# A Fourier filter and an ELU MLP on one core: order of the start's loads, place of one batch's sums, and the last unit's output

## The chip, the cores and the metric

The kernel runs on one core of a Trainium2 chip. A core has a matrix engine (TensorE, PE, with its weight loads as PEld), VectorE (DVE), ScalarE (ACT), GpSimd (POOL) and SyncE (SP), each with its own stream of instructions carried out in order, and 16 DMA engines. A DMA is issued from the stream of SP, ACT or POOL. The metric is the device time of one execution in microseconds (us); lower is better. The time before is the median of three runs, 2563.66 us (2563.2 to 2564.88).

## What is computed

`x` is (8, 3008, 256), `filt_r` and `filt_i` are (1505, 256), `moe_w_in` is (256, 2048) and `moe_w_out` (2048, 256); the two weights come in as 64-bit floats, the rest and the output as 32-bit floats.

```python
X = np.fft.rfft(x, axis=1)
F = (filt_r + 1j * filt_i)[None, :, :]
y = np.fft.irfft(X * F, n=x.shape[1], axis=1)        # (8, 3008, 256)
t = y.reshape(24064, 256)
h = t @ w_in                                          # (24064, 2048)
g = np.where(h > 0.0, h, np.exp(np.minimum(h, 0.0)) - 1.0)
out = g @ w_out                                       # (24064, 256)
```

## The kernel before

**The MLP is the bulk.** The 24064 tokens are 8 batches of 6 units (m = 0 to 5), and a unit has 4 quads (q = 0 to 3, a quarter of the 2048 hidden columns each): 192 quads in a row. In the text "quad 5" is the sixth quad of the whole run; batch 0's tokens are quads 0 to 23. The two matrix products use a seven-product scheme of Strassen's kind, so a quad has seven "up" steps (`up_steps`, matmuls of L572; they are issued as 1, 2, 6, 5, 7, 3, 4) and seven "down" steps (`down_steps`, L654), each four matmuls; the downs belong to the quad before. Between them ACT copies and exponentiates (L583, L589, L590) and DVE adds and takes the maximum (L580, L594, L630 to L634). A step that needs another product's bank waits for DVE's add of L580.

**The order is written out by hand.** The loop at the very end of the kernel issues ups and downs of a quad in a fixed pattern, "UUDUDDU" and then "DUUDUDD"; in a quad that is in the set `opens` a down goes first. Everything else is put in by `at(quad, place, function, ...)`: place 2 comes after the third step, 3 after the fifth, 0 in the middle and 1 at the end of the quad. What a function issues then stands at that place in the stream of each engine that it uses.

**The transform of the next batch runs inside the MLP of this one.** The sequence of 3008 is taken as 47 x 64. For batch b the steps are:

- `x_load` (six chunks, on SP): seven DMAs of x and of a table for each chunk.
- `x_unit` (L222, L223): two DVE operations per chunk, a sum and a difference of 128 x 512 elements.
- `a_unit` (L236): 32 matmuls for two chunks, into all four PSUM banks that the ups use too, with four evictions on ACT (L240).
- `z_write` (L310, SP): two DMAs per chunk into a scratch tensor z in DRAM; `z_read` (L316, SP): four DMAs for each of two groups of frequencies, which read z back transposed, once all of it has been written.
- `b_unit` (L385) on two groups that were read; the products with the filter (`re_mult`, `im_mult` and so on, on DVE; the filter is fetched by POOL at L326); `bi_unit` (L457); `y_write` (SP) into a scratch tensor yd.
- `tn_read` and `y_read` (L480, L491, SP) fetch a unit's inputs of the last stage, `n_unit` (L524) makes the unit's tokens, and `n_sums` (L549) the sums that the seven-product scheme needs.

Batch 0 has no MLP to hide in. Its transform and the conversion of the first weights are the start of the kernel, some 85 us: the x chunks come in by `x_load_first`, and `a_first(c)` (L279, 16 matmuls in two lots, with four evictions on ACT, L286) puts them into tiles zt. `t_first` (L298, evictions L299) transposes these, `b_first` makes the spectrum (L332) and the products with the filter (L336 to L339 on DVE), `bi_first` the way back, and the results go out and come back through DRAM (yd) to the first `n_unit` (L506).

A weight piece k is 512 KB of 64-bit floats. `w_fetch(k)` brings it in, and `step(k)` turns it to 32-bit floats: `w_split(k)` (two DVE operations), `w_float(k)` (four ACT operations), and then `w_join(k-1)` (three or four DVE operations, and `w_sums` with four more after each second piece). In the stream of ACT the evictions of `a_first` stand where they are called among the `step`s.

**SP's order in the start** is: piece 0, x chunks 0 to 2, piece 4, piece 5, chunks 3 and 4, piece 6, chunk 5, `once` (tables), `gs` (tables), piece 7. Piece 5 goes to a filter buffer, piece 6 and 7 into x buffers that `a_first` has freed. POOL fetches pieces 1 to 3 and rearranges the filter in DRAM.

**The output of a unit** is joined from the down products by seven DVE additions (L670): three at once, then two in `c_unit` and two in `o_unit`, in the order p7, c21, c12, c22. Then `o_unit` turns it with two DVE transposes (L693), one for each half k of the tokens, and issues the output DMAs (L703), 16 for most units and 24 for unit 0 of a batch. They go through SP; for the last unit, (7, 5), through SP and ACT in turn. Of the four blocks of a unit's output, c11 and c21 make up the half k = 0, c12 and c22 the half k = 1.

Of the kernel before, what the change touches and what calls it, by code (L numbers as in the profile page):

```python
# [28 lines left out]
B = 8  # L29
# [4 lines left out]
NXC = H // XC  # L34
# [99 lines left out]
def kernel(  # L134
# [9 lines left out]
    nc = tc.nc  # L144
# [497 lines left out]
    def down_steps(b, m, q):  # L642
        h = half(m)
        g = g_of.pop((b, m, q))
        if q == 0:
            po_of[b, m] = [psO.tile([P, 2, 256], FP32, tag="po%d" % i, name="po%d" % i) for i in range(4)]
        po = po_of[b, m]
        k = {}

        def step(n):  # L650
            i, u = PLACE[n]
            for a in range(2):

                nc.tensor.matmul(po[i][:, u, 0:h], w_out[q][:, COMBO[n], a, :], g[n][:, a, :],  # L654
                                 start=q == 0 and a == 0 and n in (1, 3, 6, 4), stop=True, skip_group_check=True)
            if q == 3 and n == 7:
                for i in range(2):
                    t = k[i] = kp.tile([P, 2, 256], FP32, tag="k%d" % i, name="k%d" % i)
                    nc.scalar.activation(out=t[:, :, 0:h], in_=po[i][:, :, 0:h], func=AXT.Copy)

        def tail():
            if q != 3:
                return
            p1, p5 = (k[0][:, u, 0:h] for u in range(2))
            p35, p7 = (k[1][:, u, 0:h] for u in range(2))
            c = kp.tile([P, 2, 512], FP32, tag="c", name="c")
            (c11, c12), (c21, c22) = ((c[:, i, 0:h], c[:, i, h:2 * h]) for i in range(2))

            def add(o, i0, i1):
                nc.vector.tensor_tensor(out=o, in0=i0, in1=i1, op=ALU.add)  # L670

            add(p35, p35, p5)
            add(c12, po[2][:, 1, 0:h], p1)
            add(c11, po[2][:, 0, 0:h], p1)
            rest = [(p7, p7, c12), (c21, po[3][:, 0, 0:h], p7), (c12, c12, p35), (c22, p7, p5)]
            cs_[b, m] = c, lambda i: [add(*r) for r in rest[i:i + 2]]

        return [(lambda n=n: step(n)) for n in DOWNS], tail

# [1 line left out]

    def c_unit(b, m):
        cs_[b, m][1](0)

    def o_unit(b, m):
        c, join = cs_.pop((b, m))
        join(2)
        o = op.tile([P, 16, 2, 32], FP32, tag="o", name="o")  # L690
        n = 7 if m == 0 else 8
        for k in range(2):
            nc.vector.transpose(out=o.rearrange("p (j k) e s -> p j k e s", k=2)[:, 0:n, k],  # L693
                                in_=c[:, :, k * half(m):(k + 1) * half(m)].rearrange("p e (j s) -> p j e s", s=32))

        o = o.rearrange("p (u f k) e s -> p u f k (e s)", u=4, f=2)
        queues = itertools.cycle((nc.sync, nc.scalar) if (b, m) == (B - 1, 5) else (nc.sync,))
        for k in range(2):
            for u, w, i in ((0, 3, 1), (3, 1, 0)) if m == 0 else ((0, 4, 4 * m),):
                for f in range(1 if i == 0 else 2):  # L700
                    n1 = N1 - i if f else i
                    for a in range(4):
                        next(queues).dma_start(raw(out, b * N + n1 + 32 * N1 * k,  # L703
                                                   [[N1 * D, 32], [-D if f else D, w], [1, 64]], 64 * a),
                                               o[ts(a, 32), u:u + w, f, k])

# [2 lines left out]
    def w_fetch(k, queue=nc.gpsimd):  # L711
        q, j = divmod(k, 4)

        if k in (3, 4, 14, 15):
            wd = t2[:, k % 11 - 3].rearrange("p u d -> p (u d)")
        elif k == 10:
            wd = t1p.tile([P, XC, D], FP32, tag="t1", name="wd").rearrange("p u d -> p (u d)")
        elif k in (6, 7, 8, 9):
            wd = xp.tile([P, 2, 2, D], FP32, tag="xc", name="wd").rearrange("p k u d -> p (k u d)")
        else:  # L720
            wd = fbufs[{5: 0, 11: 0, 12: 1, 13: 2}.get(k, k)].rearrange("p c u d -> p (c u d)")
        wd = wds[k] = wd.bitcast(U32).rearrange("p (a w) -> p a w", w=2)
        if j < 2:
            srcs = [moe_w_in.bitcast(U32)[ts(j, P), ts(q, 1024)]]
        else:
            srcs = [moe_w_out.bitcast(U32)[ts(4 * q + 2 * (j - 2) + i, P), :] for i in range(2)]
        for i, s in enumerate(srcs):
            n = 512 // len(srcs)
            queue.dma_start(wd[:, ts(i, n), :].rearrange("p a w -> p (a w)"), s)
# [83 lines left out]
    with tc.manual_schedule():  # L813


        with tc.tile_pool(name="boot", bufs=1) as bp:
# [37 lines left out]
            def step(k):  # L854
                w_split(k)
                w_float(k)
                if k > 0:
                    w_join(k - 1)

            for k in range(3):  # L860
                step(k)
            w_fetch(5, nc.sync)
            for c in (3, 4):
                x_load_first(c)
            a_first(0)
            w_fetch(6, nc.sync)
            x_load_first(5)
            nc.sync.dma_start(once, once_d)
            nc.sync.dma_start(gs, gs_d)
            step(3)  # L870
            for c in (1, 2):
# [2 lines left out]
                    w_fetch(c + 6, nc.sync)  # L874
            step(4)
            a_first(3)
            step(5)
            step(6)
            for c in (4, 5):
                a_first(c)  # L880
            for g in range(NG):
                f_read_first(g, ff[:, g])
                if g in (1, 3):
# [83 lines left out]
        for b in range(B):  # L967
            t = (b - 1) * PER
            if b > 0:
                for c, s in enumerate((2, 2, 3, 3, 4, 4) if b == 1 else (0, 0, 3, 3, 4, 4)):  # L970
                    at(t + s, 0, x_unit, b, c)
                    if c % 2 == 0:
                        opens.add(t + s + 1)
                        at(t + s, 1, a_unit, b, c)
                    if c % 2:
                        for k in (c - 1, c):
                            at(t + s, 1, z_write, b, k)
                        if c == NXC - 1:
                            for k in range(2):
                                at(t + s, 1, z_read, b, k)  # L980
                        for k in (c - 1, c):
                            nb, nxt = (b, k + XBUFS) if k + XBUFS < NXC else (b + 1, k + XBUFS - NXC)
                            if nb < B:
                                at(t + s, 1, x_load, nb, nxt)
                for g in range(0, NG, 2):
                    s = t + 6 + 2 * g
                    opens.update((s + 1, s + 4))
                    for k in (g, g + 1):
                        at(s - 2, 1, f_read, b, k)
                        if g:  # L990
                            at(s - 1, 0, z_read, b, k)
                    at(s, 1, b_unit, b, g)
                    at(s + 1, 2, re_mult, b, g)
                    at(s + 1, 1, re_sums, b, g)
                    parts = ((0, 0), (0, 1), (1, 0), (1, 1))
                    early = 3 if g == 6 else 4
                    at(s + 2, 2, im_mult, b, g, *parts[:early])
                    at(s + 2, 1, im_mult, b, g, *parts[early:])
                    at(s + 2, 1, im_join, b, g)
                    at(s + 3, 2, im_sums, b, g)  # L1000
                    at(s + 3, 1, bi_unit, b, g)
                    at(s + 3, 1, y_write, b, g)
            for m, s in enumerate((23, 25, 29, 32, 36, 40)):
                if b > 0 or m > 0:
                    at(t + s - 2, 0, tn_read, b, m)
                    at(t + s - 2, 1 if m == 0 else 0, y_read, b, m)
                    if b == 0 and m == 1:
                        at(t + s, 1, n_unit, b, m)
                        at(t + s, 1, n_sums, b, m)
                    else:  # L1010
                        at(t + s, 0, n_unit, b, m)
                        for place, *parts in (((t + s, 0), 0, 1, 2), ((t + s + 1, 2), 3, 4)) if m == 0 else (
                                ((t + s, 0), 0, 1), ((t + s, 1), 2, 3, 4)) if m < 3 else (((t + s + 2, 2),),):
                            at(*place, n_sums, b, m, *parts)
                if b == 0 and m == 1:
                    at(1, 1, w_join, 13)
                at(t + PER + 4 * m + 5, 0, c_unit, b, m)
                at(t + PER + 4 * m + 6, 0, o_unit, b, m)
# [57 lines left out]
```

## Time and profile before

| | |
|---|---|
| time, median of three runs | 2563.66 us (2563.2 to 2564.88) |
| the profiled execution, its own time | 2561.82 us |
| its span, first to last instruction | 2560.0 us |
| granted clock of TensorE | 0.996 |
| first matmul of the MLP | 87.39 us |
| last matmul of the MLP ends | about 2551.6 us |
| DMA traffic in the start, 0 to 40 us | 218, 313, 341, 341 GB/s in the four stretches of 10 us |

The time of an execution is the span and what lies around it, here 1.82 us. Times in the views count from the start of the span. An engine's busy share is an average over the whole span: the start, the first quads of batch 0 and the end have limits of their own, so those have to be read from their own stretches. A hole in PE's work is told by the idle time in brackets before a row, with what ended it.

### The profile page before, as it was taken

How to read it: one execution, taken by the hardware profiler on the slowest of the kernel's cores; microseconds unless marked ns; L12 is line 12 of the kernel's file. 1: busy time of each engine (PE TensorE's matmuls, PEld its weight loads, DVE VectorE, ACT ScalarE, POOL GpSimd, SP SyncE). 2: the span in 40 equal slices, each digit the busy share in tenths (PEclk: the TensorE clock that was granted, in tenths of full speed). 3: DMA queues.
4: the chain of work that ended last, by engine and by line, in shares of the span. 5: the costliest groups of instructions: out<-in, count | busy, mean ns of one | idle time of the engine just before them, and what ended most of it. 6: DMA issues, size and time to landing. Idle time of an engine off the chain costs nothing.

```text
span 2560.0 us, 43969 instructions
## 1 busy us (share of the span) xinstructions
PE 2521.4 (98%) x16682; PEld 2162.5 (84%) x16682; DVE 2067.6 (81%) x3578; ACT 1545.2 (60%) x2715; POOL 156.0 (6%) x307
## 2 busy tenths in 40 slices
PE   6999999999999999999999999999999999999998
PEld 4788889888898888988889888888889888898887
DVE  6978887788878888788877888778897788876766
ACT  7766556655566556665566655566655665555554
POOL 4001000000000000000000000000100010000000
PEclk8999999999999999999999999999999999999999
DMA  9662223523233221433225231353213322110010
GB/s 283 184 183 69 56 46 80 130 60 71 48 102 95 70 66 40 128 80 74 50 53 141 67 76 36 77 123 80 66 38 84 88 62 63 38 44 18 20 27 17
DMA packets 229879, 200.56 MB, mean 78 GB/s; under 512 B 129398, under 2 KB 201990, under 8 KB 229668
## 3 DMA queue, kind: packets, MB, share of 16 engines
q1 hardware_dynamic: 214820, 168.44, 26.9%
q0 software_dynamic: 13488, 28.86, 4.0%
q8 instruction: 131, 2.15, 0.4%
q14 instruction: 80, 0.66, 0.1%
q10 hardware_dynamic: 1360, 0.46, 0.1%
HBM read 125.80 MB, written 78.12 MB: 80 GB/s over the span
## 4 chain that ended last, share of the span: by engine, by line
PE 97%; DMA 2%; DVE 1%; issue 0%; ACT 0%; SPq 0%; DVEq 0%
PE po L654 45%; PE phs L572 25%; PE phd L572 13%; PE pha L572 6%; PE psn L524 2%; PE psa L236 2%; PE pf L385 1%; PE pv L457 1%; DMA xc<-in_x_dram 1%; PE po L332 1%; DMA x<-in_x_dram 0%; PE po L298 0%; PE psr L332 0%; PE psa L279 0%; DMA t<-yd 0%
## 5 line engine op out<-in xcount | busy, mean ns | idle before, releaser
L654 PE MATMUL po<-g,wo 128*128 128x256 f32 (+1 forms) x5376 | 1317.6, 377 | 0.0
L654 PEld LDWEIGHTS po<-g,wo 128*128 128x128 f32 x5376 | 1010.7, 190 | 165.9 <-issue 49.8
L583 ACT ACTIVATE g<-phs 128x512 f32<-128x512 f32 (+1 forms) x576 | 338.6, 588 | 735.0 <-PE phs L572 732.9
L590 ACT ACTIVATE e<-e 128x512 f32<-128x512 f32 (+1 forms) x768 | 477.1, 621 | 24.3
L594 DVE SCALAR_TENSOR_TENSOR g<-e,g 128x512 f32<-128x512 f32 (+1 forms) x576 | 387.6, 673 | 13.5 <-ACT e L590 13.1
L580 DVE TENSOR_TENSOR g<-phd,g 128x512 f32<-128x512 f32 (+1 forms) x384 | 258.9, 674 | 165.8 <-ACT e L590 108.4
L572 PE MATMUL phs<-y,wi 128*128 128x256 f32 (+1 forms) x1536 | 387.5, 375 | 0.0
L572 PE MATMUL phd<-y,wi 128*128 128x256 f32 (+1 forms) x1504 | 380.3, 375 | 0.0
L589 ACT ACTIVATE e<-g 128x512 f32<-128x512 f32 (+1 forms) x576 | 354.5, 615 | 34.2 <-DVE g L580 26.6
L572 PEld LDWEIGHTS phs<-y,wi 128*128 128x128 f32 x1536 | 291.4, 190 | 33.2 <-ACT g L583 0.2
L572 PEld LDWEIGHTS phd<-y,wi 128*128 128x128 f32 x1504 | 284.8, 190 | 35.1 <-DVE g L580 2.7
L594 DVE SCALAR_TENSOR_TENSOR g<-e,phs 128x512 f32<-128x512 f32 (+1 forms) x192 | 129.8, 676 | 115.8 <-ACT e L590 115.8
L572 PE MATMUL phs<-yt,wi 128*128 128x256 f32 (+1 forms) x768 | 193.8, 375 | 0.9 <-ACT g L583 0.9
L572 PE MATMUL phs<-yb,wi 128*128 128x256 f32 (+1 forms) x768 | 193.9, 375 | 0.6 <-ACT g L583 0.6
L572 PE MATMUL pha<-yb,wi 128*128 128x256 f32 (+1 forms) x736 | 186.0, 375 | 0.0
L589 ACT ACTIVATE e<-phs 128x512 f32<-128x512 f32 (+1 forms) x192 | 112.2, 584 | 112.0 <-PE phs L572 112.0
L580 DVE TENSOR_TENSOR g<-pha,g 128x512 f32<-128x512 f32 (+1 forms) x192 | 129.5, 674 | 44.7 <-PE pha L572 44.6
L572 PEld LDWEIGHTS phs<-yt,wi 128*128 128x128 f32 x768 | 145.7, 190 | 17.9 <-ACT g L583 1.2
L572 PEld LDWEIGHTS phs<-yb,wi 128*128 128x128 f32 x768 | 143.1, 190 | 20.2 <-ACT g L583 1.0
L326 POOL DMA_DIRECT2D fall<-fp x224 | 110.1, 499 | 719.8 <-DVE r L430 694.6
L572 PEld LDWEIGHTS pha<-yb,wi 128*128 128x128 f32 x736 | 139.3, 190 | 16.7 <-ACT fall L394 0.2
L631 DVE TENSOR_TENSOR g<-g,g 128x512 f32<-128x512 f32 (+1 forms) x192 | 130.7, 681 | 6.7
(166 smaller groups left out, 2063.5 us busy)
## 6 DMA issues: line engine op xcount, KB each, us to landing
yd<-t SPq DMA_DIRECT2D x127, 192.0 KB
t<-yd SPq DMA_DIRECT2D x92, 256.0 KB
z<-t SPq DMA_DIRECT2D x84, 256.0 KB
fall<-fp POOLq DMA_DIRECT2D x224, 96.0 KB, 2.9
t<-z SPq DMA_DIRECT2D x224, 96.0 KB
out_dram<-o SPq DMA_DIRECT2D x632, 32.0 KB
xc<-in_x_dram SPq DMA_DIRECT2D x84, 128.0 KB
xc<-in_x_dram SPq DMA_DIRECT2D x161, 64.0 KB
```

The source lines that it names most:

```text
L236: nc.tensor.matmul(p[o:o + 64, u, :], w[r, u, o:o + 64], src[r, u, :], start=True, stop=True)
L326: nc.gpsimd.dma_start(t[32 * a:32 * a + 24].rearrange("p c u d -> p (c u d)"), fp[g, a].rearrange("q c u d -> q (c u d)"))
L332: nc.tensor.matmul(ps[:, u:u + w, :], table[k, v, :], r[k, u:u + w, :], start=n == 0, stop=n == len(rhs) - 1)
L524: nc.tensor.matmul(p[ts(c, 64), dh, ts(q, 64)], t[r, i - 4 * m, ds(dh * P + 64 * c, 64)], w[r, i - 4 * m, :], start=True, stop=True)
L572: nc.tensor.matmul(ps[:, a, 0:h], w_in[q][:, COMBO[n], a, :], y[n], start=start and a == 0, stop=True, skip_group_check=True)
L580: nc.vector.tensor_tensor(out=g[o], in0=i0, in1=i1, op=ALU.add)
L583: nc.scalar.activation(out=g[o], in_=i0, func=AXT.Copy)
L589: nc.scalar.activation(out=e, in_=src, func=AXT.Relu, scale=-1.0)
L590: nc.scalar.activation(out=e, in_=e, func=AXT.Exp, scale=-1.0)
L594: nc.vector.scalar_tensor_tensor(out=g[n], in0=es[n], scalar=1.0, in1=src, op0=ALU.subtract, op1=ALU.max)
L631: nc.vector.tensor_tensor(out=b12, in0=b22, in1=b12, op=ALU.subtract)
L654: nc.tensor.matmul(po[i][:, u, 0:h], w_out[q][:, COMBO[n], a, :], g[n][:, a, :], start=q == 0 and a == 0 and n in (1, 3, 6, 4), stop=True, ...
```

## The change

Three parts that don't touch one another.

**In the start,** SP issues x chunks 3, 4 and 5 right behind piece 4, then piece 5, `once`, piece 6, `gs`, and piece 7 as before. `a_first(4)` is called before `step(5)` and `a_first(5)` between `step(5)` and `step(6)`; before, both came after `step(6)`. The orders of PE and DVE are the same as before; ACT's is changed by the place of the evictions.

**In batch 1's transform,** the six chunks' `x_unit` run at quads 2, 3, 4, 4, 5, 5 instead of 2, 2, 3, 3, 4, 4, those of quad 5 at place 2 (after its third step) and not in the middle. `a_unit`, `z_write` and the following `x_load` go to quads 3, 4 and 5 instead of 2, 3 and 4, the first two `z_read` to the end of quad 5 instead of 4, and `opens` has 4, 5, 6 instead of 3, 4, 5 for them. `b_unit(1, 0)` stays at the end of quad 6. From batch 2 on nothing is different.

**In the last unit,** the order of the last four additions is p7, c12, c22 and then c21; the half k = 1 is turned and sent out first, then c21 is added and the half k = 0 turned and sent. The 16 output DMAs go through SP, ACT and POOL in turn (6, 5 and 5) instead of SP and ACT (8 and 8).

```diff
-            cs_[b, m] = c, lambda i: [add(*r) for r in rest[i:i + 2]]
+            if last(b, m):
+                rest = [rest[i] for i in (0, 2, 3, 1)]
+            cs_[b, m] = c, lambda i, n=2: [add(*r) for r in rest[i:i + n]]
...
+    def last(b, m):
+        return (b, m) == (B - 1, 5)
...
     def o_unit(b, m):
         c, join = cs_.pop((b, m))
-        join(2)
+        join(2, 1 if last(b, m) else 2)
...
-        for k in range(2):
+        ot = o.rearrange("p (u f k) e s -> p u f k (e s)", u=4, f=2)
+        queues = itertools.cycle((nc.sync, nc.scalar, nc.gpsimd) if last(b, m) else (nc.sync,))
+        def turn(k):
             nc.vector.transpose(out=o.rearrange("p (j k) e s -> p j k e s", k=2)[:, 0:n, k],
                                 in_=c[:, :, k * half(m):(k + 1) * half(m)].rearrange("p e (j s) -> p j e s", s=32))
-        o = o.rearrange("p (u f k) e s -> p u f k (e s)", u=4, f=2)
-        queues = itertools.cycle((nc.sync, nc.scalar) if (b, m) == (B - 1, 5) else (nc.sync,))
-        for k in range(2):
+        if not last(b, m):
+            turn(0)
+            turn(1)
+        for k in (1, 0) if last(b, m) else (0, 1):
+            if last(b, m):
+                if k == 0:
+                    join(3, 1)
+                turn(k)
...
             for k in range(3):
                 step(k)
+            for c in (3, 4, 5):
+                x_load_first(c)
             w_fetch(5, nc.sync)
-            for c in (3, 4):
-                x_load_first(c)
+            nc.sync.dma_start(once, once_d)
             a_first(0)
             w_fetch(6, nc.sync)
-            x_load_first(5)
-            nc.sync.dma_start(once, once_d)
             nc.sync.dma_start(gs, gs_d)
...
             step(4)
             a_first(3)
+            a_first(4)
             step(5)
+            a_first(5)
             step(6)
-            for c in (4, 5):
-                a_first(c)
...
-                for c, s in enumerate((2, 2, 3, 3, 4, 4) if b == 1 else (0, 0, 3, 3, 4, 4)):
-                    at(t + s, 0, x_unit, b, c)
+                when = (2, 3, 4, 4, 5, 5) if b == 1 else (0, 0, 3, 3, 4, 4)
+                for c in range(NXC):
+                    s = when[c]
+                    at(t + s, 2 if s == 5 else 0, x_unit, b, c)
+                    s = when[c | 1]
                     if c % 2 == 0:
                         opens.add(t + s + 1)
                         at(t + s, 1, a_unit, b, c)
```

More of the change, by code (lines that the diff above doesn't have):

```diff
@@ L704, in o_unit @@
                                                    [[N1 * D, 32], [-D if f else D, w], [1, 64]], 64 * a),
-                                               o[ts(a, 32), u:u + w, f, k])
+                                               ot[ts(a, 32), u:u + w, f, k])
     wds = {}
```

## The prediction

> **What bounds the kernel now.** I read the page's busy times first, then the chain of waits over the start, then the timelines of the three places that the change touches. TensorE (PE) is busy for 98% of the span, so a change can only win where PE stands still: the start, a few holes, the end.
>
> ```profile
> PE 2521.4 (98%) x16682; PEld 2162.5 (84%) x16682; DVE 2067.6 (81%) x3578; ACT 1545.2 (60%) x2715; POOL 156.0 (6%) x307
> ```
>
> The chain of waits of 0 to 90 us (start, length, what) shows the start hanging on x chunks until 39.55, then on PE:
>
> ```profile
> 15.10 12.66 DMA xc<-in_x_dram
> 27.78 11.77 DMA x<-in_x_dram
> 39.68 3.77 PE psa L279 x16
> 44.00 3.57 PE po L298 x31
> ```
>
> The windows (length, then busy times; last two: DMA share and GB/s) say why: the DMA engines are full. VectorE (DVE) is the full one later in the start:
>
> ```profile
> 30.00:40.00 10.00, 6.37 (x28) 5.84 (x28) 4.28 (x8) 6.31 (x13) 3.30 (x6) 0.50 1.06 341
> 70.00:80.00 10.00, 10.00 (x60) 4.96 (x55) 9.93 (x20) 6.78 (x13) 0.00 (x0) 1.00 0.84 249
> ```
>
> The timelines (start, busy, what; in brackets the idle time before and its releaser) give the first filter product of the start, PE's two holes in quads 2 and 3 behind DVE, and DVE's idle time in quad 5:
>
> ```profile
> 48.69 0.69 DVE L336 TENSOR_TENSOR rq<-psr,ff 128x512 f32<-128x512 f32 x1 [4.21 <-PE psi L332]
> 117.63 1.02 PE L572 MATMUL phd<-yb,wi 128*128 128x224 f32 x4 [1.67 <-DVE g L580]
> 131.94 1.02 PE L572 MATMUL phd<-yb,wi 128*128 128x224 f32 x4 [0.61 <-DVE g L580]
> 158.39 0.69 DVE L549 SCALAR_TENSOR_TENSOR yb<-y,y 128x512 f32<-128x512 f32 x1 [4.93 <-ACT y L531]
> ```
>
> SP's queue, from its timeline in batch 1 and batch 2: writes of z, reads of z, output, reads of y, all in one order:
>
> ```profile
> 158.80 3.74 SPq L316 DMA_DIRECT2D t<-z  x8
> 171.34 12.24 SPq L703 DMA_DIRECT2D out_dram<-o  x24
> 184.09 1.21 SPq L491 DMA_DIRECT2D t<-yd  x2
> 466.14 3.17 SPq L316 DMA_DIRECT2D t<-z  x8
> ```
>
> And the end, where the output leaves on two queues after both transposes are begun:
>
> ```profile
> 2553.00 1.30 DVE L693 STREAM_TRANSPOSE o<-c 128x512 f32<-128x512 f32 x2
> 2553.73 3.68 SPq L703 DMA_DIRECT2D out_dram<-o  x8
> 2553.74 3.80 ACTq L703 DMA_DIRECT2D out_dram<-o  x8
> ```
>
> **The start (x ahead of w5 and w6).** Two pieces of 512 KB leave x5's path. At the 341 GB/s of the window they are 3.1 us; if POOL's queue takes half of the engines, 6.1. I take 5: x5 lands at about 34.5 instead of 39.55. What is late next: w5 comes after x5, by my estimate near 37, and ScalarE (ACT) runs in order. It makes step 5's floats (four operations, 2.6 us, as step 6's rows from 37.37 to 39.93 show), then a_first(5)'s evictions (1.2, as the rows from 39.84), then step 6's floats (2.6), then the transposes' evictions, at 37.3 + 6.4 = 43.7 against 44.55 before. PE's 32 transposes start at about 41 instead of 44.00, but fill four banks and wait for those evictions. So of 5 us about 1 arrives at the first product (L336, 48.69). It can't be more than 1.6: DVE has to do three splits (0.67 each), three joins (2.0) and one set of sums (1.7) from w5's arrival on, 9.7 us, and is free at 47.1. If w5 lands 2 us later than I think, the gain is a loss of 0.5. DVE is full from there to 80 us, so what is won at 48.69 is kept until the first MLP matmul. **-1.0 (-1.6 to +0.5).**
>
> **The sums of batch 1.** Each chunk is two DVE operations of 0.685 us. Quads 2 and 3 lose four of eight, 2.74 us, and DVE was busy 9.73 and 9.76 us of 10 from 110 to 130. But a_unit (32 matmuls, 1.89 us of PE) moves out of quad 2 as well; it was what PE did while DVE caught up, and it is still owed. By DVE's work, the matmul of 131.94 comes 2.74 earlier with 1.89 owed: -0.85. DVE wasn't quite full, and a hole may only move by a step: I take -0.5, and +0.5 as the far end. The sums in quad 5 fall into DVE's 4.93 us of idle time and cost nothing; without that cover they would cost 2.74. b>=2 is unchanged.
>
> **What follows a_unit.** a_unit(1,4) now ends with quad 5, about 162.5, not at 149.03. Behind it, on SP, come four z writes, eight z reads, then x loads, 24 output DMAs and y reads, in this order. b_unit(1,0) stays at 174.69 (14 steps of 0.865 later). Its first matmuls need all eight reads. In batch 2 the last a_unit matmul ends at 458.71, the reads issue from 466.14, and the eighth DMA behind them, which waits for the last read's lane, issues at 472.86: 14.15 us. So the reads land at 176.65 and PE stalls for **2.0**. Second: z reads start at 162.5 + 7.4 = 169.9 instead of 158.80, and all of SP's queue slips by 11.1, less 1.3 because the reads issue faster in batch 2's row. The y reads of unit (0,3), landed by 188.9 before (again by their lane), come at about 198.7; n_unit(0,3) (L524) stood at 194.61, with the first stall at 196.6. That is up to 2.1 more; or nothing, if reads with an emptier queue land 2 us sooner. I take 1.2. **Together +3.2 (0 to +5.5).** The output DMAs slip by 10 us with nothing waiting: the tile o is used again four quads later.
>
> **The end.** c12 and c22 come first, so half 1's transpose starts where c22 stood, 2552.67, and its DMAs at 2553.4 instead of 2553.73; half 0 follows at 2554.4. One more DVE operation stands between (0.33 us), hidden behind issuing. SP issues 6, at a pitch of 0.46, the last at 2555.7; the last issue before was ACT's at 2557.1, so 1.4 earlier. POOL issues 5 at 0.5 (as its gathers of the filter, L326, do), the last at 2555.4; those gathers land 2.3 to 6.5 us after issue, median 2.9: 2557.7, 2558.3 or, at worst, 2561.9. Before, the DMA engines fall silent between 2558 and 2559 (share 0.32 in that window, 0.00 in the next). Gain 0.5 to 1.1 by POOL. **-0.8 (-1.4 to +3).**
>
> [...]
>
> **Sum:** -1.0 - 0.5 + 3.2 - 0.8 = +0.9 us. The profiled execution took 2561.82 (span 2560.0), so it would take 2562.7; the median of the runs is 1.84 above it. Predicted: 2563.66 + 0.9 = **2564.6**. 0.2% is 5.1 us: faster means below 2558.5, slower above 2568.8; below that this kernel's measurement can't be told from no change.
>
> **Rivals.**
> 1. *Both holes close, no read is late.* Start -1.0, holes -2.28, end -0.8: 2559.6; with the best ends of start and end 2558.4. For it: DVE is what both holes wait for. Against: 14.15 us of z path against 12.1 us of cover, and a_unit's missing cover. Chance 0.19.
> 2. *The z path is as slow as batch 1's own: slower.* There a_unit ended at 149.03 and the DMA that takes the last read's lane issued at 167.38: 18.35 us. Then b_unit stalls for 162.5 + 18.35 - 174.69 = 6.2, z reads slip by 13.5, y reads land at 202.4 against n_unit at 200.8: 1.6 more. 7.8 in place of 3.2: **2569.2**. It decides once the z path is over 18 us. For it: DMA share 0.80 in 160 to 170. Against: in that stretch POOL's gathers and the copies of the filter ran beside the reads; they stay in quad 4 and are over. Chance 0.17.
> 3. *POOL's output is late.* At the worst landing, 6.5, the end is 3 later instead of 0.8 earlier: 2568.4. [...] Chance 0.07.
> 4. *The start loses 0.5,* since the weights become the wait on ACT and DVE: 2566.1. For it: ACT's order above leaves 0.85 us. Chance 0.10.
>
> Forecast (2562.5 to 2566.5): 0.47. Its own range is that. The range of all reaches nearly to rival 1's price and nearly to rival 2's, 2560 to 2569, and leaves out about half of each. Faster needs rival 1 at its best ends (a quarter of it): 0.05. Slower: a bit over half of rival 2: 0.10. Within 0.2%: 0.85.
>
> **What would show it.** Start: the x5 chunk in the chain ends near 34.5, L336 first runs near 47.6, L506 about 1 us before 85.36. Holes: PE's idle time before L572 in quads 2 to 4, by DVE L580, of 1.5 to 2.5 in all. Stalls: PE idle before L385 for 2 us by a z read, and before L524 of unit (0,3) for 1 us. End: the last output issues (L717) some 2 us after the last transpose has begun, instead of 3.5. I am wrong if L385 doesn't wait (rival 1), or waits for 4 us or more (rival 2); and if L336 doesn't move, the start's step has failed.

## The result and the profile after

The changed kernel takes 2569.2 us (median of 22 runs, 2564.11 to 2573.49), the kernel before, run beside it, 2564.23 (22 runs, 2561.82 to 2573.9). The ratio is 1.0014 with a 95% interval of 1.0008 to 1.0021: 3.6 us slower (2.1 to 5.4). (The medians lie 5.0 us apart, the means 3.7; the runs scatter over some 10 us, and the ratio is the figure to go by.) On the forecast's scale that is 2567.3 us. It is 0.14%, within the 0.2% that the forecast had called no change, and inside its range of all cases (2560 to 2569), but 2.7 us above its +0.9 and above the upper end of its own range (2566.5, or +2.8). The profiled execution has a span of 2567.4 us, 7.4 above that of before, more than the ratio says; why one execution can do that is seen in the start. One experiment's profiled execution (holes_by_pool) ran at a granted clock of 0.946 throughout and took 2654.89 us; its stretches are not read.

Page of the changed kernel, busy times:

```profile
PE 2524.8 (98%) x16682; PEld 2160.9 (84%) x16682; DVE 2068.3 (81%) x3578; ACT 1545.2 (60%) x2715; POOL 158.9 (6%) x312
```

The same matmuls keep PE busy for 3.4 us longer, so part of the loss is not waiting: matmuls have become slower somewhere. A cut of both traces at the first L572 of the quads tells where (us):

| stretch | before | after | difference |
|---|---|---|---|
| to the first MLP matmul | 87.22 | 90.56 | +3.34 |
| quads 0 and 1 | 20.25 | 20.29 | +0.05 |
| quads 2 and 3 | 28.93 | 28.66 | -0.27 |
| quad 4 | 13.53 | 13.53 | 0.00 |
| quads 5 and 6 | 27.31 | 29.88 | +2.56 |
| quads 7 to 9 | 38.99 | 40.39 | +1.40 |
| quad 10 to the last L654 matmul's start | 2335.02 | 2335.03 | +0.01 |
| from there to the end of the span | 8.75 | 9.07 | +0.32 |

One a_unit (1.89 us of PE) has gone from the third row to the fifth, so quads 2 and 3 really lost 1.62 and quads 5 and 6 only 0.67. Batch 1's part costs 3.7 us in all in this execution. From quad 10 to the last L654 matmul everything is the same to 0.01 us.

**The start.** The chain of waits of the changed kernel, 0 to 90 us (start, length, what), in which no x chunk stands after 10.26 us:

```profile
42.57 8.55 DMA ff<-fd
51.13 0.60 DVE zq L338
...
75.43 4.26 PE po L332 x16
```

and the timeline of DVE, its last work on weights (L784) and the first product (L336):

```profile
47.31 0.76 DVE L784 TENSOR_TENSOR wo<-wfl,we 128x256 f32<-128x256 f32 x2
49.84 0.69 DVE L336 TENSOR_TENSOR rq<-psr,ff 128x512 f32<-128x512 f32 x1 [1.76 <-PE po L298]
```

DVE was free at 48.07, PE had the spectrum at 48.08 (the end of the last psr and psi rows before it), and still the product began at 49.84. The releaser in brackets is wrong, which the chain shows: both filter rows (ff) of a product are needed, and POOL's half landed at 49.35 by its lane (the semaphore event in the trace that stands for this DMA's landing), 7.3 us after its issue. Further down, 16 matmuls of L332 that take 1.8 us elsewhere take 4.26. They stand behind a wait of 1.50 us for ACT's L364, and the granted clock, 1.00 before it, is 0.50 from 75.66 to 82.48 us by the trace's clock record (timeline of PE; window with length, busy times, granted clock, DMA share, GB/s):

```profile
75.43 2.48 PE L332 MATMUL po<-rq,gs 48*64 48x512 f32 x8 [1.50 <-ACT t L364]
```

```profile
78.00:82.00 4.00, 4.00 (x11) 1.17 (x4) 2.37 (x6) 1.81 (x3) 0.00 (x0) 0.50 0.51 145
```

**The hole of quad 3.** Timeline of PE, and the windows around it:

```profile
119.69 1.02 PE L572 MATMUL phd<-yb,wi 128*128 128x224 f32 x4 [0.34 <-DVE g L580]
...
132.67 1.02 PE L572 MATMUL phd<-yb,wi 128*128 128x224 f32 x4 [2.12 <-DVE g L580]
133.53 3.04 PE L654 MATMUL po<-g,wo 128*128 128x224 f32 x8
```

```profile
130.00:132.00 2.00, 0.55 (x3) 0.20 (x2) 1.93 (x5) 1.70 (x4) 0.00 (x0) 1.00 0.00 0
...
134.00:136.00 2.00, 2.00 (x7) 1.77 (x6) 1.93 (x4) 1.52 (x3) 0.00 (x0) 0.50 0.00 0
```

The first hole has shrunk from 1.67 to 0.34, the second has grown from 0.61 to 2.12: 2.46 in all where there were 2.28. But now the clock column falls to 0.50 behind the second, and the eight L654 matmuls there take 3.04 us where eight in a filled kernel (below) take 1.68. That is a loss that no wait list shows.

**The reads.** Timelines of PE and of SP's queue:

```profile
179.82 2.11 PE L385 MATMUL pf<-t,pairs 24*32 24x256 f32 x40
...
201.70 1.16 PE L524 MATMUL psn<-tn,t 64*64 64x64 f32 x62 [0.72 <-DMA t<-yd]
```

```profile
174.15 3.17 SPq L316 DMA_DIRECT2D t<-z  x8
...
184.63 11.84 SPq L717 DMA_DIRECT2D out_dram<-o  x24
...
196.98 1.20 SPq L491 DMA_DIRECT2D t<-yd  x2
```

b_unit doesn't stand still before its first matmul; its 40 matmuls just take 2.11 us instead of 1.72, because the later ones wait for the later reads. n_unit stops after two of its 64 matmuls until the y reads, behind the 24 output DMAs, have landed.

**The end.** Timeline, and POOL's DRAIN instructions of the program's last line with their durations (min/median/max in ns, first and last start):

```profile
2560.54 2.86 SPq L717 DMA_DIRECT2D out_dram<-o  x6
2560.55 2.35 ACTq L717 DMA_DIRECT2D out_dram<-o  x5
2560.81 2.79 POOL L717 DMA_DIRECT2D out_dram<-o  x5 [388.51 <-DVE o L702]
```

```profile
L1087 POOLq DRAIN  x3: 46/106/3896, 2562.8 to 2567.2; - x3
```

The last output lands at 2565.38 by its lane, 7.05 us after the start of the last L654 matmul, against 7.58 before: half a us won. But POOL, which now issues DMAs last of all (until 2563.6), spends 3.9 us in a DRAIN, 2562.8 to 2566.7, and the closing handshake of the engines stands behind it, 2566.7 to 2567.4. The span closes 2.0 us after the last landing; before, it took 1.2.

### The profile page after: what moved, and what is told of

It reads as the page before. It is cut to its first block, busy times and chain, and to the rows that moved or that the text cites. A ratio compares the mean times of both kernels' runs of the same rounds, so it can differ in the third digit from the quotient of the medians.

```text
span 2567.4 us, 43974 instructions
## 1 busy us (share of the span) xinstructions
PE 2524.8 (98%) x16682; PEld 2160.9 (84%) x16682; DVE 2068.3 (81%) x3578; ACT 1545.2 (60%) x2715; POOL 158.9 (6%) x312
## 4 chain that ended last, share of the span: by engine, by line
PE 95%; DMA 2%; DVE 1%; ACT 1%; SPq 0%; issue 0%; POOL 0%; POOLq 0%; ACTq 0%; DVEq 0%
PE po L654 45%; PE phs L572 25%; PE phd L572 13%; PE pha L572 6%; PE psn L524 2%; PE psa L236 2%; PE pf L385 1%; PE pv L457 1%; DMA t<-in_moe_w_in_dram 1%; PE po L332 0%; DMA fall<-in_moe_w_in_dram 0%; SPq L717 0%; DMA ff<-fd 0%; DMA xc<-in_x_dram 0%; DMA yd<-t 0%
## 5 line engine op out<-in xcount | busy, mean ns | idle before, releaser
L654 PE MATMUL po<-g,wo 128*128 128x256 f32 (+1 forms) x5376 | 1319.0, 377 | 0.0
L654 PEld LDWEIGHTS po<-g,wo 128*128 128x128 f32 x5376 | 1011.6, 190 | 166.1 <-issue 49.7
L580 DVE TENSOR_TENSOR g<-phd,g 128x512 f32<-128x512 f32 (+1 forms) x384 | 259.0, 674 | 169.5 <-ACT e L590 111.2
L572 PE MATMUL phs<-y,wi 128*128 128x256 f32 (+1 forms) x1536 | 387.7, 375 | 0.5 <-ACT y L507 0.5
L572 PE MATMUL phd<-y,wi 128*128 128x256 f32 (+1 forms) x1504 | 380.3, 375 | 0.0
L572 PEld LDWEIGHTS phs<-y,wi 128*128 128x128 f32 x1536 | 291.3, 190 | 34.2 <-ACT y L507 0.7
L572 PEld LDWEIGHTS phd<-y,wi 128*128 128x128 f32 x1504 | 284.8, 190 | 35.1 <-DVE g L580 2.7
L572 PE MATMUL phs<-yt,wi 128*128 128x256 f32 (+1 forms) x768 | 193.9, 375 | 0.9 <-ACT g L583 0.9
L572 PE MATMUL phs<-yb,wi 128*128 128x256 f32 (+1 forms) x768 | 193.9, 375 | 0.6 <-ACT g L583 0.6
L572 PE MATMUL pha<-yb,wi 128*128 128x256 f32 (+1 forms) x736 | 186.0, 375 | 0.0
L580 DVE TENSOR_TENSOR g<-pha,g 128x512 f32<-128x512 f32 (+1 forms) x192 | 129.5, 674 | 47.2 <-PE pha L572 47.2
L572 PEld LDWEIGHTS phs<-yt,wi 128*128 128x128 f32 x768 | 145.7, 190 | 18.0 <-ACT g L583 1.5
L572 PEld LDWEIGHTS phs<-yb,wi 128*128 128x128 f32 x768 | 143.1, 190 | 20.2 <-ACT g L583 1.0
L572 PEld LDWEIGHTS pha<-yb,wi 128*128 128x128 f32 x736 | 139.3, 190 | 16.7
```

The costliest lines, as they stand in the source:

```text
L572: nc.tensor.matmul(ps[:, a, 0:h], w_in[q][:, COMBO[n], a, :], y[n], start=start and a == 0, stop=True, skip_group_check=True)
L580: nc.vector.tensor_tensor(out=g[o], in0=i0, in1=i1, op=ALU.add)
```

## The experiments

Each ran in turn with the kernel before on the same chip; a ratio is to that. "Quad 1 to quad 10" is from first L572 to first L572. It took 122.30 us in each profiled execution without batch 1's part or another edit of quads 1 to 9 (before, start_alone, end_alone, start_light, start_rows_sp), and 125.99 in the changed kernel, so a tenth of a us can be read there, which no time of a whole run allows.

**The three parts alone.** The diffs are those of the change, one part at a time.

> Only the start's part of the change. In the changed kernel's trace the MLP begins (first L572 of the first quad) at 90.56 us against 87.22 before, 3.3 late. Theory 'POOL's half of the first filter rows': the first ff read on POOL lands late (49.35 against 47.05) because the queues are full there, and the y writes behind it too; then this kernel alone begins its MLP at 89 to 91 us and takes +2 to +3.5 us, though x chunk 5 is in at about 36.7 instead of 39.55. Rival 'chance': the start of any one execution scatters by some us; then the time is within 1 us of before and L572 begins at 86 to 88. Rival 'as forecast': -1 us.

Ratio 0.9999 (0.9991 to 1.0008). The MLP began at 90.11 and L336 at 48.93. Seven profiled executions without the start's part began it at 87.2 to 90.6 us, mean 88.8, with L336 at 48.5 to 50.3. 'Chance' fits the time, though not its 86 to 88 us for the MLP. A gain of 1 us lies within the interval (-2.3 to +2.1 us), so the time doesn't exclude it, but the trace doesn't show it; the loss of 2 to 3.5 us isn't there.

> Only batch 1's part. Theory 'clock': from the first L572 of quad 0 to that of quad 10 it takes 132.7 us instead of 129.0 (+3.7), of which 1.4 to 1.5 are matmuls at a granted clock of 0.50 after one hole of 2.1 us in quad 3, about 1.0 the wait for the y reads at L524, 0.4 the wait in L385; the time is +3 to +4 us. Rival 'reads': all of the loss is at L385 and L524, 3 us, and the clock stays at 1.00. Rival 'interplay': without the late start the DMA queues are free again, the reads are in time, and the time is +0 to +1.5.

Ratio 1.0010 (1.0001 to 1.0019), +2.6 us: this part carries the result. Quad 1 to quad 10 took 127.36, 5.1 more than before, but in the longest execution of its runs (2571.36 us; median 2567.39), and quad 0 took 1.0 more. The hole is the same as in the changed kernel, and so is the clock behind it:

```profile
133.74 1.50 PE L572 MATMUL phd<-yb,wi 128*128 128x224 f32 x4 [2.12 <-DVE g L580]
```

```profile
134.00:136.00 2.00, 2.00 (x7) 1.80 (x7) 1.46 (x4) 1.21 (x3) 0.00 (x0) 0.54 0.00 0
```

The wait at L524 was longer here (1.31 + 0.75 us). By itself that doesn't rule out 'interplay', since this execution's MLP began late too, at 90.62; but in the two filled runs below it began at 88.81 and 88.16, and the wait at L524 was 1.5 and 1.4 us. The late reads need no late start.

> Only the last unit's part. Theory 'close': the last output lands 0.5 us earlier after the last matmul (7.05 us after the last L654 group's start against 7.58), but with POOL's DMAs the span closes 2.0 us after the last landing instead of 1.2, so the time is +0.1 to +0.5. Rival 'landing': the close was chance, and the time is -0.4 to -0.9. Neither can be told from no change by the time alone; the profile's end decides.

Ratio 0.9999 (0.9991 to 1.0008). From the last L654 matmul's start to the end 9.1 us again, with the same DRAIN. Before the change that DRAIN stood behind POOL's last gather at 2164, where nobody waits (first fence: end_alone, second: before):

```profile
L1085 POOLq DRAIN  x3: 46/93/3897, 2556.3 to 2560.7; - x3
```

```profile
L1071 POOLq DRAIN  x3: 51/93/4737, 2164.1 to 2559.8; - x3
```

**The hole filled, twice.** Batch 1's part, and five matmuls into a free bank, whose result nobody uses, right before the last up step of quad 3:

```diff
+                if i == 3 and k == "U" and len(ups) == 1:
+                    fill(5)
                 if s:
                     s.pop(0)()
```

> Batch 1's part, with five more matmuls of 512 columns (about 2.2 us of PE, into a free bank, their result unused) right before the last up step of quad 3, where PE stands still for 2.1 us. Theory 'clock': PE has something to do in the hole, the granted clock stays at 1.00 through quad 3, and from quad 0 to quad 10 it takes 1.2 to 1.5 us less than with batch 1's part alone, although PE does 2.2 us more work. Rival 'reads' or 'the hole alone': no clock is lost there, so the filled kernel takes the same or up to 0.5 us longer.

Five of 512 columns took 4.46 us, twice the hole. The clock stayed at 1.00, but quad 3 took 17.73 us and the ratio was 1.0015 (1.0006 to 1.0024): the fill was mis-sized, so it showed the clock and not its price. With 256 columns:

> Batch 1's part alone with the hole of quad 3 filled by five matmuls of 256 columns (about 2.2 us). The fill of 512 columns took 4.46 us, so it kept the clock at 1.00 but was itself 2.2 us too long (quad 3 took 17.73 us against 17.51 unfilled). Theory 'clock': quad 3 now takes 15.4 to 15.8 us, 1.7 to 2.0 less, with the clock at 1.00; from quad 1 to quad 10 it takes 2 us less than batch 1's part alone under the same waits at L524. Rival 'the hole alone': DVE sets the end of quad 3, which then takes 17.4 to 17.8 whatever PE does in the hole.

```profile
127.97 2.32 PE L687 MATMUL fill<-wi 128*128 128x256 f32 x10
130.26 1.02 PE L572 MATMUL phd<-yb,wi 128*128 128x224 f32 x4
131.12 1.68 PE L654 MATMUL po<-g,wo 128*128 128x224 f32 x8
```

```profile
130.00:132.00 2.00, 2.00 (x11) 1.75 (x10) 1.91 (x5) 1.18 (x3) 0.00 (x0) 1.00 0.00 0
```

Quad 3 took 15.82 us, 1.69 less than unfilled, with 2.3 us more work on PE. The wait for DVE is the same; what is gone is the half clock. Quad 1 to quad 10 took 125.13. 'The hole alone' is out. The ratio, 1.0008 (0.9999 to 1.0016), can't be told from that of the unfilled run: the 1.69 us are read in one execution of each.

**The y reads ahead of the output.** As hole_filled, and:

```diff
-                    at(t + s - 2, 0, tn_read, b, m)
-                    at(t + s - 2, 1 if m == 0 else 0, y_read, b, m)
+                    early = (b, m) == (0, 3)
+                    at(t + s - (3 if early else 2), 1 if early else 0, tn_read, b, m)
+                    at(t + s - (3 if early else 2), 1 if m == 0 or early else 0, y_read, b, m)
```

> The same, and tn_read and y_read of unit (0, 3) moved from quad 6's middle, behind 24 output DMAs, to the end of quad 5, ahead of the z writes. Theory 'queue': they are in before n_unit needs them, no wait stands at L524, quad 8 takes 13.4 us as before the change (14.5 to 15.8 with it), and from quad 1 to quad 10 it takes 122.8 to 123.4 us, against 122.3 before the change. Rival 'z reads': the y reads push the z path back by their 1.2 us, L385 waits that much longer and half of the gain is lost.

```profile
178.10 1.75 PE L385 MATMUL pf<-t,pairs 24*32 24x256 f32 x14
180.11 1.13 PE L385 MATMUL pf<-t,pairs 24*32 24x256 f32 x26 [0.27 <-DMA t<-z]
```

The wait at L524 is gone (quad 8 took 13.38, as before the change), but b_unit now takes 3.1 us instead of 2.3 (hole_filled), and quad 6 15.45 instead of 14.58. Of the 1.77 us won in quad 8, 0.87 went back there: the rival 'z reads' was half right. Quad 1 to quad 10 took 124.24 (122.8 to 123.4 expected), the ratio is 1.0006 (0.9997 to 1.0014). On the one queue, the y reads were early at the cost of the z reads.

**What makes the holes.**

```diff
-                                    (2, 2, w_sums, 13), (2, 1, w_join, 14), (2, 1, w_join, 15),
-                                    (3, 0, w_sums, 15, nc.vector, (0, 1, 2)), (3, 1, w_sums, 15, nc.vector, (3,))):
+                                    (2, 2, w_sums, 13, nc.gpsimd), (2, 1, w_join, 14), (2, 1, w_join, 15),
+                                    (3, 0, w_sums, 15, nc.gpsimd, (0, 1, 2)), (3, 1, w_sums, 15, nc.gpsimd, (3,))):
```

> The kernel before, with two edits. First, the weight sums of pieces 13 and 15 (eight DVE additions, 3.4 us, in quads 2 and 3) go to GpSimd, which took 3.04 us for four such sums in the start. If both holes of quads 2 and 3 (1.67 and 0.61 us) are there because DVE has too much to do, both close and quad 1 to quad 10 takes 120.0 to 120.8 us instead of 122.3. Rival: GpSimd is late with the sums, or slows DVE, and a wait of the same size stands in quads 2 to 4. Second, the last unit goes out in two halves in turn, on SP and ACT alone. Theory 'POOL's drain': without POOL's DMAs the span ends 8.4 to 8.6 us after the start of the last L654 matmul (8.75 before, 9.1 with POOL); rival 'turn': the two halves themselves lengthen the end and it stays at 8.9 or more. Together -2 to -2.5 us.

The second edit, the end on SP and ACT, is as in light_end below. Ratio 0.9996 (0.9986 to 1.0007): the 2 us don't show, and the interval (-3.6 to +1.8 us) doesn't exclude them. The holes are read from all_three, which has the same two edits.

> The kernel before, with the weight sums of pieces 13 and 15 on GpSimd and chunk 0's sums of batch 1 in quad 1 instead of quad 2; a_unit stays in quads 2 to 4, so nothing behind it is late. DVE loses 3.05 us (1.68 and 1.37) before the first hole of 1.67 us, and 1.7 before the second. Theory 'DVE throughput': both holes close, quad 1 to quad 10 takes 120.0 to 120.4 us instead of 122.3, the time is -1.9 to -2.5 us. Rival 'latency': the hole is the time from the sum of the matmul to the next matmul behind x sums issued just before, and only the 1.37 us of them counts: 120.9 to 121.2. [...]

Ratio 0.9994 (0.9985 to 1.0003); quad 1 to quad 10 took 121.67, 0.6 less than before, not 2. Quad 2 lost 1.94 us, but quad 1 gained 0.83 and quad 3 0.47.

> What looked useful, together: the start's part with piece 10's DMAs later and the first filter group on SP, the weight sums of pieces 13 and 15 on GpSimd (x sums as before the change), the last unit in two halves on SP and ACT. By the parts: the start -1 (-3 to +1), the holes -0.7 to -1.7, the end -0.3: -2 to -5 us. If the start's scatter of some 3 us hides it, the time is within 1 us of before, and the quads' own times (quad 1 to quad 10: 120.6 to 121.6) tell.

Ratio 1.0048 (1.0036 to 1.0061), 12 us slower, by the start (the MLP began at 101.55; see start_rows_sp). The end, on SP and ACT, took 8.44 us after the last L654 matmul's start. Quad 1 to quad 10 took 122.71 (120.6 to 121.6 expected). Its x sums of batch 1 lie as in the kernel before, and both holes were still there, 1.75 and 0.93 us, although eight additions had gone from DVE to GpSimd. Timelines of DVE and POOL of all_three:

```profile
127.24 1.00 DVE L222 TENSOR_TENSOR sd<-xc 128x512 f32<-128x512 f32 x1
128.27 1.10 DVE L223 TENSOR_TENSOR xc<-xc 128x512 f32<-128x512 f32 x1
129.30 1.21 DVE L222 TENSOR_TENSOR sd<-xc 128x512 f32<-128x512 f32 x1
```

```profile
126.96 4.14 POOL L798 TENSOR_TENSOR wi<-wi 128x256 f32<-128x256 f32 x4 [54.96 <-DVE wi L781]
```

The x sums take 1.00 to 1.21 us beside GpSimd's additions instead of 0.69, and these take 4.14 for four instead of 3.04: what one engine is spared, both pay. From the first L572 of quad 2 to the end of the L580 that ends the second hole DVE was busy for 24.24 us, where it was 23.70 before, so this run doesn't show what less work on DVE would do to the holes. The sums went back to DVE in the last run.

**The start again.** start_light issues piece 10's DMAs in the loop over the filter groups, at the third (g = 2); start_rows_sp changes one queue:

```diff
-        for a, (r, queue) in enumerate(((LO, nc.gpsimd), (HI, nc.sync))):
+        for a, (r, queue) in enumerate(((LO, nc.sync if g == 0 else nc.gpsimd), (HI, nc.sync))):
```

> The start's part alone, with the DMAs of weight piece 10 (512 KB) issued by POOL some 9 us later, after the third group of filter products. Theory 'bytes': the start is set by the DMAs that all y writes queue behind; with 512 KB less in front the first y write lands 1.5 to 2 us earlier than in start_alone (64.61 there by its lane, 63.67 to 65.5 over the runs), PE doesn't wait 1.9 us for an eviction at 73 us (L332 behind L364), and the MLP begins at 87 to 88.5 us instead of 90.1. Rival 'filter rows': the first product (L336 at 48.5 to 49.9 in all runs) sets it, nothing moves but by chance, and the MLP begins at 88 to 91.

Ratio 0.9991 (0.9981 to 1.0001); the MLP began at 88.63. But the first y write landed at 64.88, not earlier, so 'bytes' isn't borne out, and 88.63 is no better than the mean without the part. Inconclusive.

> The start's part alone, with both halves of the first filter group (ff) read through SP; POOL reads the other seven halves as before. In three executions with the start's part PE had the first spectrum at 47.3 to 47.9 us and DVE was free at 47.3 to 48.0, as forecast, but the first product (L336) began at 48.9 to 50.3, 0.5 us after POOL's half of ff had landed (48.5 to 49.8; 47.05 in the execution that the forecast read). Theory 'filter rows': with that half on SP it lands by 46, and L336 begins at 47.5 to 48.2. It says no more than that of the time: a second limit, the y writes behind the other reads (they land at 64 to 66 us in all runs), lets the MLP begin at 88 to 90.5 all the same, and the time stays within 2 us of before. Rival 'it carries': what L336 gains, 1 to 2 us, is found at the first L572 and in the time.

Ratio 1.0041 (1.0027 to 1.0054), 10 us slower. Chain of waits:

```profile
35.42 17.95 DMA ff<-fd x2
...
53.89 0.69 DVE rq L336
```

POOL's other seven reads, which stand behind the first one's wait for the rearranged filter where that one is on POOL (issued at 40.84 in start_alone), now went out from 35.42 on; SP's reads of the first group, issued at 39.54 and 40.11, were done at 51.81 and 53.36 behind them. What was expected of the landing was wrong. But L336 followed the filter rows to 53.89, and the MLP followed to 97.03: the filter rows do set the first product, and one that is 5.0 us later than in start_alone costs 6.9 there. (PE stood for 4.99 us, and the clock was 0.50 from 53.59 to 67.25.)

**All that seemed worth keeping.** start_light, chunk 0's x sums in quad 1 (a_unit left in place), the end on SP and ACT (the first piece against the kernel before, the second against the changed kernel):

```diff
-                    at(t + s, 0, x_unit, b, c)
+                    at(t + s - (1 if b == 1 and c == 0 else 0), 0, x_unit, b, c)
...
-        queues = itertools.cycle((nc.sync, nc.scalar, nc.gpsimd) if last(b, m) else (nc.sync,))
+        queues = itertools.cycle((nc.sync, nc.scalar) if last(b, m) else (nc.sync,))
```

> The kernel before, with the start's part and piece 10's DMAs issued later (as in start_light), chunk 0's sums in quad 1 with a_unit left in quads 2 to 4 and the weight sums left on DVE, and the last unit in two halves on SP and ACT. The sums on GpSimd are left out, since DVE's x sums took 1.00 to 1.21 us beside them instead of 0.69. Theory 'what stands just before': quad 2's hole is the x sums that DVE has to do just ahead of the add that PE waits for, so with two fewer it falls from 1.67 to 0.3 and quad 2 takes 13.9 to 14.1 us instead of 15.37; quad 1 pays up to 0.6 for them; quad 1 to quad 10 takes 121.0 to 121.8 us (122.3 before). Rival 'throughput': the hole moves to quad 3 as in the change, 2 us long, and 122.0 to 123.5 is taken. The end: 8.4 to 8.6 us from the last L654 matmul's start to the span's end. The start: the MLP begins at 87 to 90 us, by chance mostly. Time -1 to -4 us.

Ratio 0.9995 (0.9986 to 1.0004), median 2563.11 us against 2564.37. It is faster than the changed kernel, but can't be told from the kernel before. Its parts by the trace: quad 2 took 13.97 us (13.9 to 14.1 expected), quad 1 paid 0.84, quad 1 to quad 10 took 121.76, so 0.54 is won, and the hole did not move on to quad 3 (13.56). The end took 8.51 us after the last L654 matmul's start: without POOL's DMAs some 0.25 less than before, 0.6 less than with them. Its profiled execution was the longest of its runs, 2572.05 us (the others 2562.16 to 2565.45), and shows why one execution can be so late (timeline of PE; windows):

```profile
52.20 1.32 PE L332 MATMUL psr<-tf,once 48*64 48x512 f32 x2 [1.73 <-DVE rq L337]
```

```profile
50.00:60.00 10.00, 8.27 (x37) 3.57 (x35) 7.24 (x13) 3.17 (x6) 1.14 (x2) 0.64 1.03 250
60.00:70.00 10.00, 10.00 (x45) 4.81 (x48) 5.04 (x10) 4.63 (x9) 3.38 (x5) 0.50 0.41 111
```

A product waited for its filter row, PE stood for 1.73 us, the clock went to 0.50 and stayed there through 60 to 70 us, and the MLP began at 97.34.

## Where the prediction held, and where its terms were wrong

**The start: forecast -1.0, measured 0 (-2.3 to +2.1 by start_alone's interval).** Everything up to the product came as forecast: x5 landed at 36.7 instead of 39.55 (34.5 forecast), and in the changed kernel PE and DVE were both ready at 48.1 (47.6 and 47.1). What failed is the step "So of 5 us about 1 arrives at the first product". It left out that the product also needs POOL's half of the filter, which landed at 47.05 in the one execution that was read. The step counted two of three inputs. In the seven executions of the unchanged start that half landed at 47.1 to 49.4, and in four of them the product waited for PE, not for it; in the four with x ahead (changed kernel, start_alone, start_light, light_end) PE was ready at 47.4 to 48.2, that half landed at 48.5 to 50.4, and the product began 0.47 to 0.50 us after it each time. By the forecast's own sign ("if L336 doesn't move") the step has failed. That what is won at L336 is kept until the MLP isn't borne out for a us or so either: an L336 at 50.30 went with an MLP at 88.63 (start_light), one at 48.93 with 90.11 (start_alone). The +3.3 of the changed kernel's profile is within what unchanged starts scatter (87.2 to 90.6), most of it the slow L332 matmuls at a clock of 0.50.

**The holes: forecast -0.5 (far end +0.5), measured +1.6 in the profiled execution.** Two steps failed. The first is the count "2.74 earlier with 1.89 owed: -0.85", from which the -0.5 was taken. It left out a part of the change: quad 3 is no longer in `opens`, so one down step (four L654 matmuls) that stood ahead of the second hole now stands behind it. From quad 2's first L572 to that hole PE has 48 L654 matmuls to do instead of 52 and no a_unit, and is busy for 19.35 us instead of 22.19: 2.84 less, not 1.89. The L580 that ends the hole comes 21.76 us after the same point instead of 24.41: 2.65 less, nearly the 2.74 of the forecast. The holes grow by the difference, 0.2, from 2.28 to 2.46 us. So it is DVE's work up to the hole, less PE's, that makes them; in light_end, with 1.37 us off DVE ahead of the first hole and PE's order unchanged, the holes are 0.27 and 0.61, 1.4 less. This is a sum of one execution's rows; a run with the down step put back was not made. The second step that failed is that holes were priced by their length alone. One hole of 2.12 instead of 1.67 and 0.61 took the clock with it, and hole_filled puts that at 1.69 us. Both profiled executions that had this hole unfilled paid it (the changed kernel's and that of sums_alone); in how many others the clock fell was not shown.

**The reads: forecast +3.2 together, measured about 0.4 at L385, 1.0 at L524 and 0.7 in small delays around them in the changed kernel (2.1).** The two waits are where the forecast put them, for the reasons given. The first is smaller for two reasons. The z path itself took 13.2 us (167.6, the end of a_unit, to 180.76) against 14.15. And "Its first matmuls need all eight reads" is not so: 14 of the 40 ran before the last read was there (reads_early's rows), which gives it that much longer to land. The second scattered: 0.72 here, 2.1 in sums_alone, 1.5 and 1.4 in the filled runs.

**The end: forecast -0.8, measured +0.3.** The landing came 0.5 earlier, within the 0.5 to 1.1 of "by POOL". The step that failed is that the span ends with the last landing as before: POOL's DRAIN of 3.9 us, which no row of the trace's end had shown, took its place. Of the forecast's rivals this is nearest to the third, but not by a late landing: POOL's DMAs themselves landed 2.1 to 2.5 us after issue.

**The sum.** Of the four terms only the reads came out with the sign that was forecast. The misses are +1.0 at the start, +2.1 at the holes, -1.1 at the reads and +1.1 at the end. They don't cancel: they add up to +3.1 in the profiled stretches and +2.7 in the time. That the total stays inside the range of all is owed to the width of that range, which was drawn for the rivals, and is luck as far as the terms go. No rival came true. The second's direction did, at two thirds of its price (3.6 of 5.5 us) and by other means: its stall of 6.2 us at L385 was 0.4. That the median of the runs reads 2569.2, rival 2's figure, is chance.

## What to carry to other kernels

Price a hole in front of PE by what it does to the clock, not by its length alone: 1.67 and 0.61 us left it at 1.00 here, 2.46 us as 0.34 and 2.12 did not. Work moved out of a place also takes away the cover that it gave there: count every step that changes sides of the hole, on both engines. List every input of the instruction that a chain is to speed up, and take the landing times of its DMAs from more than one execution. Before a DMA goes to another queue, look at what that queue's instructions were holding back, and at the end of the program at what that engine still has to finish.

## What the runs showed of the hardware

- **The length of a hole alone does not say whether the clock falls.** The hole of 2.12 us in quad 3 was followed by a clock of 0.50 in both runs that had it (133.68 to 137.10 in the changed kernel, 3.41 us; 0.54 over 134 to 136 in sums_alone), and what the fill won back was 1.69 us. Before the first L506, holes of 2.18 (sums_filled, a clock of 0.70 over 84 to 88) and 3.17 us (sums_alone, 0.50 over 88 to 92) were followed by a lower clock. The 2.80 us of the kernel before were not (1.00 from 43.32 to 2555.53), nor were the 2.71 us that PE stood in hole_filled between 80 and 90 (1.00 from 50 to 100). One of 1.73 us in light_end (0.50 over 55 to 60) and one of 1.50 in the changed kernel's start (0.50 from 75.66) were. In the traces of the kernel before and the changed kernel the stretches between two changes of the clock that are under 60 us long are 3.41 (three), 6.83 (two), 13.65, 37.55 and 51.20 us: 1, 2, 4, 11 and 15 times 3.413. What decides whether a hole costs the clock was not shown.
- **Where GpSimd issued DMAs last, its DRAIN stood at the end of the program:** it took 3896 (the changed kernel) and 3897 ns (end_alone) and ended 3.1 us after its last issue and 1.3 us after the last landing.
- **DVE additions beside GpSimd additions were slower,** in all_three between 1.00 and 1.21 us each instead of 0.69, and so were GpSimd's, 4.14 instead of 3.04 us for four. Why was not shown.
